# A written order of 431 steps for every engine, over units 0 to 8 of an attention and two-layer kernel

## The chip, the cores and the metric

One core of a Trainium2 chip runs the program. The metric is device time in microseconds, the median of repeated executions. The engines are TensorE (PE; its weight loads are PEld), VectorE (DVE), ScalarE (ACT), GpSimd (POOL) and SyncE (SP), which here only issues DMAs. Each engine works through its own instructions strictly in the order in which they stand in its list, and waits for the others by semaphores.

## What is computed

```python
q_pool = q.reshape(B, H, S // 2, 2, D).mean(axis=3)          # B 4, H 8, S 1152, D 64
scores = (1 / sqrt(D)) * q_pool @ k.transpose(0, 1, 3, 2)    # 576 x 1152 per head
attn = softmax(scores)                                       # maximum taken off first, sum + 1e-9
x = (attn @ v) as [2304 tokens, 512]
h = x @ w_in                                                 # 512 x 2048
g = where(h >= 1, h, where(h <= -1, 0, (h + 1) ** 2 / 4))
y = g @ w_out                                                # 2048 x 512
out = maximum(y @ w1, y @ w2, y @ w3) @ w_out2               # 512 x 768 (three), 768 x 512
```

Weights arrive as 64-bit floats; q, k and v as 32-bit floats.

## The kernel before

The attention is cut into 48 units (b, i, p): batch, third of the pooled queries (192 of them), pair of heads. A unit has three score groups, named by `who` 0, 1 and 2: 128 queries of one head, 128 of the other, and the last 64 of both. For each group PE makes 128 x 1152 scores `sc` (line 371), DVE takes the row maximum into `st` (385), ACT scales it (386) and takes the exponential into `pf` with the row sum in `sm` (387). PE turns `pf` in nine pieces into `tr` (423), ACT copies that to `pt` (434, 436), and PE multiplies `pt` with v (`av`, 454). Score and turned tiles share two places of three PSUM banks each (`place`, 148); all else that PE writes there shares two banks of the tag `g1`. `shares` (393) makes 1/sum: DVE inverts `sm`, POOL spreads it into `rb`, PE turns it (403, 404) into the tail of the place that holds `tr` of group 2, and ACT copies it to `R` (406, 407). Only then is that place free for a new `sc`. DVE multiplies `av` with `R` into `xf` (472); after four units the batch row block becomes `xh`, and the dense work begins: `ph` (523) with w_in and `py` (546) with w_out, eight `ph` and four `py` to a block of 192 tokens. `py` needs every half of w_out.

Beside the first units the weights are made. w_in comes in eight chunks of 1 MB (`raw_in`, 185), w_out in eight chunks of two loads of 512 KB each. ACT makes a chunk's absolute value (161), DVE turns it to 32 bits in four instructions (162, 163, 165, 167), ACT squares it for a norm (199, 252), and when the scale is known ACT and DVE make a high and a low half of 16 bits (153, 154). For w_out the scale needs the norms of all eight chunks and a turn on PE, `max_ou` (108). Five of the chunks of w_out, the third and the last four, are loaded into one tile `raw_ou` (238), so each of these loads waits until the second DVE instruction of line 167 of the one before has ended. k (and q) of a pair are squared on ACT (285), summed over partitions on PE (101), scaled and split on POOL and DVE (274, 275), and turned by a DMA into `kst` (and `qst`); v of batch 0 is used whole.

Before the change PE alone has a written order: the table `ORDER` gives the words of a unit, for the first 12 units

```python
"s0 w0 r d s1 d w1 t0 a1 q t1 w2 s2 d d w3 t2"
```

with `s` the scores and softmax of a group, `t` its turn, `r` 1/sum of the unit before, `a1` the `av` of the unit before, `d` one step of the dense work (from unit 5 on), `w` one step of the weights, which `W_AT` admits at some places only, and `q` the next q. `K0` and `V0` say at which group k and v of batch 0 take a step. PE's instructions stand as these words make them. The lists of the other engines are arranged by the framework's own scheduler, which goes by priorities; `shift(OW)` moves the weights' priority back.

Of the kernel before, what the change touches and what calls it, by code (L numbers as in the profile page):

```python
# [50 lines left out]
def body(ctx: ExitStack, tc: tile.TileContext, q, k, v, w_in, w_out, w1, w2, w3, w_o2, out):  # L51
# [28 lines left out]
    @contextmanager  # L80
    def shift(n):
        n = max(n, -tc.cur_priority)
        tc.cur_priority += n
        yield
        tc.cur_priority -= n

# [83 lines left out]
    def w_in_steps():  # L170
# [4 lines left out]
        HF = FF // 2  # L175

        f32 = wou.rearrange("p a b c d -> p (a b c d)").bitcast(F32)
        sqs = wou.rearrange("p a b c d -> p (a b c d)")[:, NF * DM:].rearrange("p (k f) -> p k f", k=KD).bitcast(BF16)
        raws = []

        def fetch(n):
            if n < 2 * KD:
                kt, h = divmod(n, 2)
                raw = gp.tile([P, HF, 2], U32, tag="g", name=f"raw_in{kt}_{h}")
                issued["w"] = load_q.dma_start(out=raw, in_=words(w_in[kt * P:(kt + 1) * P, h * HF:h * HF + HF])).ins
                raws.append(raw)

        fetch(0)
        yield
        fetch(1)  # L190
        yield
        for kt in range(KD):
            st = f32[:, kt % 2 * FF:(kt % 2 + 1) * FF]
            for h in range(2):
                c = slice(h * HF, h * HF + HF)
                raw = raws.pop(0)
                to_f32(st[:, c], raw)
                fetch(2 * kt + h + 2)
                nc.scalar.activation(out=sqs[:, kt, c], in_=st[:, c], func=AF.Square,
                                     accum_out=sq[:, 2 * kt + h:2 * kt + h + 1])  # L200
                if h == 0:
                    yield
            nc.vector.tensor_tensor(out=sr[:, kt:kt + 1], in0=sq[:, 2 * kt:2 * kt + 1], in1=sq[:, 2 * kt + 1:2 * kt + 2],
                                    op=ALU.add)
            root_scale(u_in[:, kt:kt + 1], s[:, kt:kt + 1], sr[:, kt:kt + 1], 1)
            for h in range(2):
                c = slice(h * HF, h * HF + HF)
                split_rows(win[:, 0, kt, c], win[:, 1, kt, c], st[:, c], s[:, kt:kt + 1])
            yield

        ps = psg.tile([P, 512], F32, tag="g1", name="sum_in")
        for kt in range(KD):
            for c in range(4):
                nc.tensor.matmul(ps[32 * c:32 * c + 32], ones16, sqs[:, kt, c * 512:(c + 1) * 512],
                                 start=(kt == 0), stop=(kt == KD - 1))
        nc.vector.tensor_reduce(out=um[:, 2:3], in_=ps, axis=AX.X, op=ALU.max)
# [3 lines left out]
        all_max(U_in, um, 2, "in")  # L220
        yield

    def w_ou_steps():
        NG = NF // 2
        mx = small.tile([P, NG], F32, tag="wsq", bufs=1, name="mx_ou")
        um = small.tile([P, 2], F32, tag="um", bufs=1, name="um_ou")
        s = small.tile([P, 1], F32, tag="wsc2", bufs=1, name="s_ou")
        f32 = wou.rearrange("p a b c d -> p a (b c d)").bitcast(F32)

        sts = [f32[:, h + 1] for h in range(NG - 1)]  # L230
        one = gp.tile([P, 6, DM], U32, tag="g", name="raw_ou")
        sts.append(one[:, 4:6].rearrange("p a b -> p (a b)").bitcast(F32))
        raws = {}

        def fetch(h):
            at_ = {0: 6, 1: 4, 3: 6}.get(h)
            if at_ is None:
                raw = one[:, 0:4].rearrange("p (a c) b -> p a (c b)", c=2).rearrange("p a (b c) -> p a b c", c=2)
            else:
                raw = wou[:, at_:at_ + 2].rearrange("p a b c d -> p a (b c d)").bitcast(U32).rearrange(  # L240
                    "p a (b c) -> p a b c", c=2)
            for f in range(2):
                ff = 2 * h + f
                load_q.dma_start(out=raw[:, f], in_=words(w_out[ff * P:(ff + 1) * P, :]))
            raws[h] = raw

        for h in range(3):
            fetch(h)
        yield
        for h in range(NG):  # L250
            to_f32(sts[h], raws.pop(h).rearrange("p a b c -> p (a b) c"))
            nc.scalar.activation(out=wou[:, 0, 0].bitcast(BF16), in_=sts[h].rearrange("p (a b) -> p a b", a=2),
                                 func=AF.Square, accum_out=mx[:, h:h + 1])
            for x in {0: (3,), 2: (4,), 4: (5,), 5: (6,), 6: (7,)}.get(h, ()):
                fetch(x)
            yield
        nc.vector.tensor_reduce(out=um[:, 0:1], in_=mx, axis=AX.X, op=ALU.max)
        root_scale(um[:, 1:2], s, um[:, 0:1], 1)
        all_max(U_ou, um[:, 1:2], 1, "ou")
        nc.vector.reciprocal(out=s, in_=U_ou)  # L260
        for h in range(NG):
            split_rows(wou[:, h, 0], wou[:, h, 1], sts[h].rearrange("p (a b) -> p a b", a=2), s)
            if h % 2:
                yield
# [7 lines left out]
    def split(hi, lo, x, s):  # L272

        nc.gpsimd.tensor_scalar(out=hi, in0=x, scalar1=s, scalar2=1.0, op0=ALU.mult, op1=ALU.mult)  # L274
        nc.vector.scalar_tensor_tensor(out=lo, in0=x, scalar=s, in1=hi, op0=ALU.mult, op1=ALU.subtract)

# [5 lines left out]
    def norm(n, junk, j, b, p, key):  # L282

        sq = small.tile([P, 1], F32, tag="sq", bufs=2, name=f"sq{key}{b}_{p}")
# [3 lines left out]
        root_scale(ub[b][:, p, j:j + 1], sb[b][:, p, j:j + 1], all_add(sq, 1, f"{key}{b}_{p}"), 1)  # L288

    def k_steps(b, p):  # L290

        if p == 0:
            ub[b] = small.tile([P, NPAIR, 2], F32, tag="ub", bufs=3, name=f"ub{b}")
            sb[b] = small.tile([P, NPAIR, 2], F32, tag="sb", name=f"sb{b}")
# [6 lines left out]
        split(kp[:, :, 0], kp[:, :, 1], kn.rearrange("p a b c -> p (a b) c"), sb[b][:, p, 0:1])  # L301
# [3 lines left out]
    def v_steps(b, p):  # L305

        if WHOLE(b, p):
# [6 lines left out]
            yield  # L314
# [6 lines left out]
        split(vv[:, 0], vv[:, 1], vn.rearrange("p a b c -> p (a b c)"), sb[b][:, p, 1:2])  # L321
        yield

    def q_prep(b, i, p):
# [543 lines left out]
```

## Time and profile before

| what | value |
|---|---|
| median of 3 runs | 1209.26 us (1209.18 to 1212.24) |
| the profiled execution | 1203.48 us |
| its span in the trace | 1201.7 us |
| mean granted clock of TensorE over the span | 0.956 |
| busy over the span: PE, DVE, ACT, POOL | 1074.7, 822.1, 739.6, 139.1 us |
| first `py` of the dense work | 229.65 us after the span's start |

Times in the trace count from the start of the span; the profiled execution is 1.8 us longer than its span, and 5.8 us shorter than the median of the runs. A window of the trace gives each engine's busy time and the granted clock of TensorE in it, where 1.00 is 2.4 GHz and a stretch in between mixes 2.4 and 1.2 GHz. The first maximum of a unit (line 385) marks where a unit begins below.

### The profile page before, as it was taken

The page shows a single profiled execution, that of the slowest core. Times are in us where ns is not written, and L with a number is a line of the kernel's source. Part 1 is how long each engine was busy: PE and PEld are TensorE (multiplying, and loading weights), DVE is VectorE, ACT ScalarE, POOL GpSimd, SP SyncE. Part 2 cuts the span into 40 slices and gives each one's busy share as a digit, 9 for nine tenths or more (in the row PEclk, how much of TensorE's full clock was granted, in tenths as well). Part 3 has the DMA queues.
Part 4 walks back from the last instruction along what each step waited for, and adds up shares of the span by engine and source line. Part 5 has one row for each costly group of instructions (what it writes and reads, how often), then busy time and mean ns, then how long its engine had stood idle before and what let it go on. Part 6 is the DMA issues. An engine that isn't in the chain of part 4 may idle for free.

```text
span 1201.7 us, 26667 instructions
## 1 busy us (share of the span) xinstructions
PE 1074.7 (89%) x11061; PEld 883.2 (73%) x11061; DVE 822.1 (68%) x1404; ACT 739.6 (62%) x1337; POOL 139.1 (12%) x160
## 2 busy tenths in 40 slices
PE   3557787899899988999999899998988999999998
PEld 2344566778788877788878788887986876777774
DVE  4976866668788888888889988786998551422220
ACT  4875777677777877777877888776474311112111
POOL 1110002112011121110112200000401020100000
PEclk9768889899999999999999999999988999999999
DMA  7854232247766689865589765556444120000001
GB/s 236 250 157 132 80 127 54 70 103 153 145 113 115 120 175 183 172 114 113 113 169 192 154 101 100 100 92 161 139 155 138 41 69 27 10 19 19 19 18 45
DMA packets 273754, 134.91 MB, mean 112 GB/s; under 512 B 229088, under 2 KB 256736, under 8 KB 272608
## 3 DMA queue, kind: packets, MB, share of 16 engines
q1 hardware_dynamic: 273632, 133.20, 48.8%
q8 instruction: 87, 1.43, 0.5%
q14 instruction: 35, 0.29, 0.1%
HBM read 62.39 MB, written 9.44 MB: 60 GB/s over the span
## 4 chain that ended last, share of the span: by engine, by line
PE 44%; DVE 4%; ACT 3%; issue 3%; DMA 3%; POOL 0%; ACTq 0%; SPq 0%; POOLq 0%; DVEq 0%
PE p L767 18%; PE py L546 7%; PE po L784 5%; PE ph L523 5%; PE sc L371 4%; PE av L459 3%; PE tr L423 1%; DMA pt<-hl 1%; DVE st L385 1%; ACT pf L387 1%; PE por L798 1%; ACT hl L440 1%; DVE st_m L167 1%; DVE hl L441 0%; DMA raw_m<-in_moe_w_dram 0%
## 5 line engine op out<-in xcount | busy, mean ns | idle before, releaser
L385 DVE TENSOR_REDUCE st<-sc 128x1 f32<-128x1152 f32 x144 | 194.6, 1351 | 45.5 <-PE sc L371 45.1
L767 PE MATMUL p<-yh,wm 128*128 128x288 f16 x1728 | 217.9, 288 | 5.7 <-ACT py L550 3.2
L371 PE MATMUL sc<-kst,qst 128*64 128x512 f16 (+3 forms) x1152 | 177.0, 341 | 39.3 <-ACT R L407 17.6
L546 PE MATMUL py<-g,wou 128*128 128x192 f16 x2304 | 204.3, 250 | 7.6 <-DVE xf L472 4.2
L767 PEld LDWEIGHTS <-wm 128*128 128x128 f16 x1728 | 170.2, 99 | 53.1 <-issue 7.0
L546 PEld LDWEIGHTS <-wou 128*128 128x128 f16 x2304 | 195.2, 100 | 15.9 <-issue 15.0
L523 PE MATMUL ph<-xh,win 128*128 128x192 f16 x2304 | 203.9, 249 | 3.2 <-POOL xh L274 2.1
L523 PEld LDWEIGHTS <-win 128*128 128x128 f16 x2304 | 195.2, 99 | 5.9 <-issue 3.5
L387 ACT ACTIVATE pf<-sc,st,esc 128x1152 f32<-128x1152 f32 x144 | 188.8, 1311 | 5.8
L371 PEld LDWEIGHTS <-qst 128*64 128x64 f16 (+1 forms) x1152 | 84.6, 108 | 99.7 <-issue 42.5
L423 PE MATMUL tr<-ident,pf 128*128 128x128 f32 x648 | 97.9, 304 | 50.4 <-ACT pf L387 50.4
L423 PEld LDWEIGHTS tr<-ident,pf 128*128 128x128 f32 x648 | 82.0, 158 | 61.7 <-ACT pf L387 55.4
L441 DVE TENSOR_TENSOR hl<-pf,hl 128x1152 f16<-128x1152 f32 x72 | 100.2, 1391 | 13.4 <-ACT hl L440 10.7
L775 ACT ACTIVATE h<-mx 128x288 f16<-128x288 f32 x48 | 21.2, 443 | 133.5 <-DVE mx L773 133.5
L772 DVE TENSOR_TENSOR mx<-p,mx 128x288 f32<-128x288 f32 x48 | 21.9, 456 | 106.2 <-PE p L767 105.7
L459 PE MATMUL av<-pt,vhl 128*64 128x192 f16 x1944 | 87.1, 247 | 3.7 <-DMA pt<-hl 3.7
L459 PEld LDWEIGHTS <-vhl 128*64 128x64 f16 x1944 | 79.3, 110 | 13.4 <-issue 8.3
L386 ACT ACTIVATE st<-st,esc 128x1 f32<-128x1 f32 x144 | 41.6, 289 | 71.2 <-DVE st L385 70.7
L440 ACT ACTIVATE hl<-pf 128x1152 f16<-128x1152 f32 x72 | 83.1, 1154 | 0.0
L531 DVE SCALAR_TENSOR_TENSOR g<-t,dgs,g 128x384 f16<-128x384 f32 x96 | 62.3, 653 | 5.0 <-ACT g L530 4.9
L784 PE MATMUL po<-wo,h 128*128 128x512 f16 x288 | 64.3, 379 | 0.0
L430 DVE TENSOR_TENSOR pt<-tr,pt 128x1152 f16<-128x1152 f32 x36 | 48.8, 1356 | 18.8 <-ACT pt L429 18.8
(171 smaller groups left out, 1267.3 us busy)
## 6 DMA issues: line engine op xcount, KB each, us to landing
kn<-in_k_dram SPq DMA_DIRECT2D x16, 576.0 KB, 4.4
vn<-in_v_dram SPq DMA_DIRECT2D x16, 576.0 KB, 4.3
raw_m<-in_moe_w_dram SPq DMA_DIRECT2D x12, 768.0 KB, 4.5
raw_in<-in_moe_w_in_dram SPq DMA_DIRECT2D x8, 1024.0 KB, 5.9
qn<-in_q_dram SPq DMA_DIRECT2D x24, 256.0 KB, 3.4
raw_ou<-in_moe_w_out_dram SPq DMA_DIRECT2D x10, 512.0 KB, 4.4
qst<-qst SPq DMA_DIRECT2D x48, 96.0 KB, 2.2
y_d<-ys SPq DMA_DIRECT2D x48, 96.0 KB, 2.0
```

The costliest lines, as they stand in the source:

```text
L371: nc.tensor.matmul(sc[m0:m1, n0:n1], qst[b, i, p][who][:, var, m0:m1], ks[:, h, n0:n1], start=(var == 0), stop=(var == 1))
L385: nc.vector.tensor_reduce(out=m, in_=sc, axis=AX.X, op=ALU.max, negate=True)
L387: nc.scalar.activation(out=pf, in_=sc, func=AF.Exp, bias=nb, scale=e, accum_out=sums[b, i, p][:, who:who + 1])
L423: nc.tensor.transpose(tr[:, c * P:(c + 1) * P], pf[:, c * P:(c + 1) * P], ident)
L440: nc.scalar.activation(out=hl[:, 0], in_=pf, func=AF.Copy)
L441: nc.vector.tensor_tensor(out=hl[:, 1], in0=pf, in1=hl[:, 0], op=ALU.subtract)
L459: nc.tensor.matmul(acc[64 * h:64 * h + 64], vhl[b, p][:, vi, h, c, :], pt[:, h, pi * KT + c, :], start=(c == 0 and e == 0), stop=(c == KT ...
L523: nc.tensor.matmul(ph[:, a], win[:, wi, kt, ff * P:(ff + 1) * P], x[:, xi, kt], start=(kt == 0 and e == 0), stop=(kt == KD - 1 and e == 2))
L531: nc.vector.scalar_tensor_tensor(out=g[:, 1, fs, :], in0=t2, scalar=gs, in1=g[:, 0, fs, :], op0=ALU.mult, op1=ALU.subtract)
L546: nc.tensor.matmul(py, wou[:, ff // 2, wi, ff % 2, m * P:(m + 1) * P], g[:, gi, ff, :], start=(ff == 0 and e == 0), stop=(ff == NF - 1 and ...
L767: nc.tensor.matmul(ph[:, :NB2], wm[:, wi, i, kt, ff * P:(ff + 1) * P], yh[:, yi, kt, n0:n0 + NB2], start=(kt == 0 and e == 0), stop=(kt == ...
L784: nc.tensor.matmul(po, h2t[b][:, hi, ff, t * P:(t + 1) * P], wo[:, wi, ff, :], start=(ff == 0 and e == 0), stop=(ff == NF2 - 1 and e == 2))
```

## The change

Units 0 to 8 are no longer made by `ORDER`. A string `OPENING` of 431 steps names pieces of work, and each mention of a piece runs it to its next `yield`: `v0` to `v3` and `k0` to `k3` (v and k of batch 0), `q0` to `q8`, `w0` to `w7` and `wi` (chunks of w_in, and its scale), `o0` to `o7` and `oo` (chunks of w_out, and its scale), `sNW` (group W of unit N, from the scores to the copy into `pt`), `rN` (1/sum), `aN` (`av`), `x0`, `x1` (`xh` of a block) and `u00` to `u06` (the first seven `ph` of the dense work). While this runs, PE, ACT, DVE, POOL and SP all take their instructions in the order in which the steps make them; the scheduler may still put instructions of later units between them, and does on ACT, DVE, POOL and SP. 1/sum of these units is turned into a bank of the tag `g1` (`rs`), no longer into the tail of `tr`. The scaled maximum of these units is made on DVE. From unit 9 on the table `ORDER` goes on without the words for the weights; seven `ph` are done by then, before it was eight.

```diff
+OTHERS = {mybir.EngineType.Activation, mybir.EngineType.DVE, mybir.EngineType.Pool, mybir.EngineType.SP}
+FROM = 9
+FIRST = lambda b, i, p: b == 0 and 4 * i + p < FROM
+NB_DVE = (0, 1, 2)
+OPENING = """
+v0 v1 q0 v2 v3 v0 k0 q2 v0 v1 v0 q0 v1 w0 v1 w1 q0 k1 v2 q0 q0 v2 v3 q0 v2 q0 v3 k0 v3 q4 q2 k0 k0 q2 k0 q2 w0
...
+r7 s72 o4 s80 r7 s81 s80 o4 o5 a7 s81 s80 s80 s81 a7 x1 x1 u05 s80 o5 x1 s81 u05 o5 s82 s81 u05 u06 s82 u05 u05
+s82 o5 u06 o5 o6 s82 u06 s82 u06 u06 o6 o6 o6 o7 o6 o7 o7 o7 o7 oo oo oo o0 o0 o1 o1 o2 o2 o3 o3 o4 o4 o5 o5 o6
+o6 o7 o7
+"""
...
     def soft(b, i, p, who):
...
+        sc = qk(b, i, p, who)
+        yield
...
+        nc.vector.tensor_reduce(out=m, in_=sc, axis=AX.X, op=ALU.max, negate=True)
+        if FIRST(b, i, p) and who in NB_DVE:
+            nc.vector.tensor_scalar(out=nb, in0=m, scalar1=e, scalar2=PS, op0=ALU.mult, op1=ALU.add)
+        yield
+        if not (FIRST(b, i, p) and who in NB_DVE):
+            nc.scalar.activation(out=nb, in_=m, func=AF.Copy, scale=e, bias=PS)
         pf = pfp.tile([P, KT * P], F32, tag="pf", name=f"pf{key}")
...
+        yield from turned(b, i, p, who, pf)
...
     def shares(b, i, p):
...
+        rs = R[b, i, p] if not FIRST(b, i, p) else psg.tile([P, 512], F32, tag="g1", name=f"rs{b}_{i}_{p}")
         nc.tensor.transpose(rs[:, 0:P], rb.rearrange("p a o -> p (a o)"), ident)
...
+    def opening():
+
+        gens = {}
+        for name in OPENING.split():
+            if name not in gens:
+                gens[name] = piece(name)
+            run(gens[name], 1)
+        for name in gens:
+            run(gens[name])
...
     order = tc.manual_schedule(engines=ORDERED)
     order.__enter__()
...
+    with tc.manual_schedule(engines=OTHERS):
+        opening()
+    for t in range(3 * FROM):
+        now(t)
...
+    for n, (b, i, p) in list(enumerate(units))[FROM:]:
```

Where the change moves instructions, three places, as the built programs list them. Names carry unit and group: `sc0_0_1_0` is group 0 of unit (0, 0, 1).

PE at the end of unit 0, before:

```order
L371 MATMUL sc0_0_0_2_237<-kst0_0_125,qst0_0_0_149 64x128
L423 MATMUL tr0_0_0_2_278<-ident_80,pf0_0_0_2_251 128x128 x9
L371 LDWEIGHTS qst0_0_0_149
L371 MATMUL sc0_0_1_0_291<-kst0_1_181,qst0_0_0_149 128x512
L371 LDWEIGHTS qst0_0_0_149
```

and in the change:

```order
L394 MATMUL sc0_0_1_0_353<-kst0_1_229,qst0_0_0_188 128x128
L106 MATMUL sum_k0_3_377<-sqk0_3_367,ones_78 128x1
L458 MATMUL tr0_0_0_2_384<-ident_80,pf0_0_0_2_375 128x128 x9
L458 MATMUL tr0_0_1_0_402<-ident_80,pf0_0_1_0_382 128x128 x9
L433 MATMUL rs0_0_0_416<-ident_80,rb0_0_0_400 128x128
L434 MATMUL rs0_0_0_416<-ident_80,sm0_0_0_281 128x128
```

The turn of group 2 stood right behind its scores; now the scores of the next unit's group 0 stand between, two turns follow each other, and 1/sum goes to a tile of its own.

DVE from the first chunk of w_in to the first two maxima, before:

```order
L162 TENSOR_SCALAR wou_74<-wou_74 128x1024
L163 TENSOR_SCALAR wou_74<-wou_74 128x1024
L165 SCALAR_TENSOR_TENSOR wou_74<-raw_in0_0_157,wou_74 128x1024
L167 SCALAR_TENSOR_TENSOR wou_74<-raw_in0_0_157,wou_74 128x1024
L385 TENSOR_REDUCE st0_0_0_0_172<-sc0_0_0_0_165 128x1
L385 TENSOR_REDUCE st0_0_0_1_193<-sc0_0_0_1_186 128x1
```

and in the change, behind the whole first chunk and the first half of the second:

```order
L173 SCALAR_TENSOR_TENSOR wou_74<-raw_in0_1_165,wou_74 128x1024
L175 SCALAR_TENSOR_TENSOR wou_74<-raw_in0_1_165,wou_74 128x1024
L282 SCALAR_TENSOR_TENSOR kpre0_1_228<-kn0_1_170,sb0_123,kpre0_1_228 128x18x64
L207 TENSOR_TENSOR sr_in_157<-sq_in_156 128x1
L98 TENSOR_SCALAR u_in_77<-sr_in_157 128x1
L100 TENSOR_SCALAR u_in_77<-u_in_77 128x1
L101 RECIPROCAL s_in_158<-u_in_77 128x1
L379 SCALAR_TENSOR_TENSOR esc0_0_0_279<-ub0_122,sqq0_0_0_168 128x1
L409 TENSOR_REDUCE st0_0_0_0_282<-sc0_0_0_0_258 128x1
L411 TENSOR_SCALAR st0_0_0_0_282<-st0_0_0_0_282,esc0_0_0_279 128x1
L409 TENSOR_REDUCE st0_0_0_1_287<-sc0_0_0_1_272 128x1
```

Two chunks and the second k stand ahead of the first maximum, where one chunk stood, and the scaled maximum follows each maximum.

PE around the turn of w_out's scale, before (in unit 7):

```order
L454 MATMUL av0_1_2_1462<-pt_0_1_2_1258,vn0_2_434 64x192 x18
L423 MATMUL tr0_1_3_1_1499<-ident_80,pf0_1_3_1_1409 128x128 x9
L108 MATMUL max_ou_1514<-ident_80,um_ou_890 128x128
L371 LDWEIGHTS qst0_1_2_1094
L371 MATMUL sc0_1_3_2_1522<-kst0_3_437,qst0_1_2_1094 64x512
```

and in the change (behind unit 8):

```order
L567 MATMUL ph0_0_6_1621<-xh0_0_996,win_73 128x192
L458 MATMUL tr0_2_0_2_1660<-ident_80,pf0_2_0_2_1651 128x128 x9
L113 MATMUL max_ou_1695<-ident_80,um_ou_1689 128x128
L394 LDWEIGHTS qst0_2_0_1095
L394 MATMUL sc0_2_1_0_1720<-kst0_1_229,qst0_2_0_1095 128x512
```

The turn now stands behind the last group of unit 8, right ahead of the first scores of unit 9. The eight low halves of w_out (line 154, now 258) had all stood ahead of unit 9's first maximum in DVE's list; in the change one stands ahead of it and seven behind.

## Rows read from the trace of the kernel before

**Rows 1.** Stretches: span, length, busy PE, PEld, DVE, ACT, POOL, PEclk, DMA share, GB/s.

```profile
20.10:40.00 19.90, 13.36 (x57) 9.18 (x55) 16.49 (x27) 17.13 (x26) 1.52 (x2) 0.84 1.02 345
40.00:131.50 91.50, 55.19 (x382) 38.69 (x382) 69.74 (x137) 64.13 (x100) 12.35 (x15) 0.76 0.50 143
131.50:217.90 86.40, 65.20 (x551) 52.28 (x552) 59.57 (x98) 65.87 (x107) 10.48 (x13) 0.86 0.30 90
217.90:229.65 11.75, 11.75 (x124) 9.74 (x123) 6.57 (x11) 9.19 (x16) 1.00 (x1) 0.99 0.12 36
229.65:800.00 570.35, 543.74 (x6723) 478.15 (x6723) 475.97 (x775) 443.30 (x834) 78.32 (x99) 0.99 0.70 135
```

**Rows 2.** Waits of PE up to 215.7 us: total us, times, longest.

```profile
PE tr L423 <- ACT pf L387: 43.8, 14, 8.9
...
PE sc L371 <- ACT R L407: 8.0, 3, 4.0
```

**Rows 3.** Timeline of PE in 185:206: start, us, instructions, idle time before.

```profile
185.50 1.20 PE L423 MATMUL tr<-ident,pf 128*128 128x128 f32 x9
...
191.13 2.18 PE L423 MATMUL tr<-ident,pf 128*128 128x128 f32 x9 [3.22 <-ACT pf L387]
193.10 1.69 PE L371 MATMUL sc<-kst,qst 128*128 128x512 f16 x6
...
199.18 1.14 PE L371 MATMUL sc<-kst,qst 128*128 128x512 f16 x6 [2.17 <-ACT R L407]
```

**Rows 4.** Timeline of DVE at the start.

```profile
6.88 0.15 DVE L95 TENSOR_SCALAR ub<-ub 128x1 f32<-128x1 f32 x1
7.07 0.16 DVE L96 RECIPROCAL sb<-ub 128x1 f32<-128x1 f32 x1
...
9.02 1.42 DVE L275 SCALAR_TENSOR_TENSOR kpre<-kn,sb,kpre 128x1152 f16<-128x1152 f32 x1
10.93 0.62 DVE L275 SCALAR_TENSOR_TENSOR qpre<-qn,sqq,qpre 128x384 f16<-128x384 f32 x1 [0.49 <-POOL qpre L274]
11.46 0.69 DVE L162 TENSOR_SCALAR wou<-wou 128x1024 f32<-128x1024 f32 x1
...
14.17 1.22 DVE L167 SCALAR_TENSOR_TENSOR wou<-raw_in,wou 128x1024 uint32<-128x1024 uint32 x1
20.10 1.36 DVE L385 TENSOR_REDUCE st<-sc 128x1 f32<-128x1152 f32 x1 [4.71 <-PE sc L371]
```

**Rows 5.** Timeline of DVE in 50:60.

```profile
51.46 1.27 DVE L154 SCALAR_TENSOR_TENSOR win<-wou,s_in,win 128x1024 f16<-128x1024 f32 x1
52.65 0.68 DVE L163 TENSOR_SCALAR wou<-wou 128x1024 uint32<-128x1024 uint32 x1
...
58.25 1.34 DVE L385 TENSOR_REDUCE st<-sc 128x1 f32<-128x1152 f32 x1
59.52 1.20 DVE L165 SCALAR_TENSOR_TENSOR wou<-raw_in,wou 128x1024 uint32<-128x1024 uint32 x1
```

**Rows 6.** Timeline of DVE in 164:175.

```profile
165.76 1.22 DVE L167 SCALAR_TENSOR_TENSOR wou<-raw_ou,wou 128x1024 uint32<-128x1024 uint32 x1
166.90 0.61 DVE L531 SCALAR_TENSOR_TENSOR g<-t,dgs,g 128x384 f16<-128x384 f32 x1
167.43 0.55 DVE L529 SCALAR_TENSOR_TENSOR t<-t 128x384 f32<-128x384 f32 x1
167.90 0.41 DVE L472 SCALAR_TENSOR_TENSOR xf<-av,Uv,R 128x192 f32<-128x192 f32 x1
...
173.07 0.69 DVE L162 TENSOR_SCALAR raw_ou<-raw_ou 128x1024 f32<-128x1024 f32 x1 [1.32 <-ACT raw_ou L161]
```

**Rows 7.** Timeline of ACT in 164:175.

```profile
171.90 1.14 ACT L161 ACTIVATE raw_ou<-raw_ou 128x1024 f32<-128x1024 f32 x1 [0.56 <-DMA raw_ou<-in_moe_w_out_dram]
```

**Rows 8.** Page, costliest groups: the scaled maximum on ACT.

```profile
L386 ACT ACTIVATE st<-st,esc 128x1 f32<-128x1 f32 x144 | 41.6, 289 | 71.2 <-DVE st L385 70.7
```

**Rows 9.** Timeline of ACT at the start.

```profile
4.75 1.16 ACT L285 ACTIVATE kpre<-kn 128x1152 bf16<-128x1152 f32 x1 [2.74 <-DMA kn<-in_k_dram]
```

More of the change, by code (lines that the diff above doesn't have):

```diff
@@ L219, in w_in_steps @@
         yield
-        all_max(U_in, um, 2, "in")
+        yield from all_max(U_in, um, 2, "in")
         yield
-    def w_ou_steps():
-        NG = NF // 2
-        mx = small.tile([P, NG], F32, tag="wsq", bufs=1, name="mx_ou")
-        um = small.tile([P, 2], F32, tag="um", bufs=1, name="um_ou")
[L227 to L248, printed above, removed]
-        yield
[L250 to L259, printed above, removed]
@@ L260, in w_ou_steps, with w_ou_last @@
+    def w_ou_last():
+        um = small.tile([P, 2], F32, tag="um", bufs=1, name="um_ou")
+        s = w_s["ou"] = small.tile([P, 1], F32, tag="wsc2", bufs=1, name="s_ou")
+        nc.vector.tensor_reduce(out=um[:, 0:1], in_=w_s["mx"], axis=AX.X, op=ALU.max)
+        root_scale(um[:, 1:2], s, um[:, 0:1], 1)
+        yield
+        yield from all_max(U_ou, um[:, 1:2], 1, "ou")
         nc.vector.reciprocal(out=s, in_=U_ou)
[L261 to L264, printed above, removed]
+        yield
@@ new lines, in down_step @@
+        for ff in range(NF):
+            for e, (wi, gi) in enumerate(((0, 0), (0, 1), (1, 0))):
+                nc.tensor.matmul(py, wou[:, ff // 2, wi, ff % 2, m * P:(m + 1) * P], g[:, gi, ff, :],
+                                 start=(ff == 0 and e == 0), stop=(ff == NF - 1 and e == 2))
+        yield
+        ys = tp.tile([P, NB], F32, tag="ys", bufs=1, name=f"ys{b}_{i}_{m}")
+        nc.scalar.activation(out=ys, in_=py, func=AF.Copy, scale=gd)
+        nc.scalar.activation(out=py, in_=py, func=AF.Square, scale=gd, accum_out=y2[:, b, i, m:m + 1])
@@ L554, in dense_steps @@
+        copy_q.dma_start(out=y_d[b][:, m, i * NB:(i + 1) * NB], in_=ys)
+        yield
+    begun = set()
     def dense_steps(units):
-        down = iter(())
+        down = []
         for b, i in units:
-            for k, _ in enumerate(up_steps(b, i)):
-                yield
-                if k % 2 == 1:
-                    next(down, None)
+            for k in range(NF // 2):
+                if ("u", b, i, k) not in begun:
+                    run(up_step(b, i, k))
                     yield
-                    yield
-            down = down_steps(b, i)
@@ L565, in dense_steps @@
-        for _ in down:
+                if k % 2 == 1 and down:
+                    job = down.pop(0)
+                    if ("y", *job) not in begun:
+                        run(down_step(*job))
+                        yield
+                        yield
+            down = [(b, i, m) for m in range(NM)]
+        for job in down:
+            run(down_step(*job))
             yield
             yield
-    def run(gen):
-        for _ in gen:
-            pass
     dense = dense_steps([(b, i) for b in range(B) for i in range(NBL)])
-    def w_steps():
-        yield from w_in_steps()
-        yield from w_ou_steps()
```

368 lines of the change are left out of this document (213 added, 155 removed).

## The prediction

> **What bounds the kernel now.** I read first the busy time by stretches. Behind the first `py`, at 229.65 us, PE is busy for 543.74 of 570.35 us, 95%; before it, in units 1 to 8, for 55.19 of 91.50 and 65.20 of 86.40 us, 60% and 75% [rows 1]. From the first `py` on PE's list is the same in both kernels but for the `ph` done ahead, so what the change is worth is by how much the first `py` moves. Next come the waits of PE ahead of it: the largest by far is that for the exponential, `tr` on `pf`, 43.8 us in 14 waits; `sc` on `R` has 8.0 in 3 [rows 2]. The timeline of PE shows the pattern: scores of one group, a turn that must wait 3.22 us for that group's maximum and exponential, the next scores, a wait of 2.17 us for `R` [rows 3]. Last, DVE: it is busy 69.74 of 91.50 and 59.57 of 86.40 us [rows 1], the busiest engine in the first and, behind PE and ACT, not far off in the second. So a unit lasts as long as DVE's instructions in it, plus what a serial round leaves open.
>
> I sum DVE's list with prices taken from start to start, since neighbours overlap a little: a small instruction 0.19 us (6.88 to 7.07); a chunk of weights 3.93 (11.46 to the end of its fourth instruction, 14.17 + 1.22), the low half of a k 1.42, of a q 0.53 [rows 4]; a 16-bit half of a chunk 1.19 (51.46 to 52.65), a maximum 1.27 (58.25 to 59.52) [rows 5]; one `g` 0.53, one second step of `t` 0.47, one `xf` 0.33 of its 0.41 as an estimate [rows 6]. Units 1 to 4 of before hold 12 maxima (15.2), 72 small (13.7), 16 half chunks of two instructions (31.4), 8 halves (9.5) and 6.8 of the rest: 76.6 of 91.5 us. Units 5 to 8 hold 61.2 of 86.4. What is left is 14.9 and 25.2 us: **the overhead of a unit is 3.7, then 6.3 us**, 5.0 on average. These are the two numbers that the change can alter.
>
> **The change part by part.**
>
> *The written order.* In units 1 to 7 DVE's new list holds 21 maxima (26.7), 21 scaled maxima and 69 other small ones (17.1), ten chunks (38.8), seven halves (8.3) and 13.7 of the rest (a k, four q, seven `xf`, an `xh`, five steps of the dense work): **104.6 us**. Scores now go in pairs: two in flight, then two turns, so that one group's maximum and exponential lie beside the other's turn and copy. Three rounds of a unit become one and a half, even units with one pair and odd ones with two. I take the overhead as halved with them: 1.85 a unit for units 1 to 4, 3.15 for 5, 6, 7 and 9, in all 7.4 + 12.6 = **20.0 us**. Bounds: nothing at all below, and 6.3 a unit above, as in units 5 to 8 now; I take the half because the count of rounds is what changes.
>
> *1/sum in its own bank.* The 8.0 us of `sc` on `R` [rows 2] lie in the overhead that was halved; nothing more is counted. Covering it is the next wait, that for `pf`. The bank is one of the two of `g1`, which the sums of k and v, `av` and `ph` share; each of those is held for one copy, so a delay is bounded by a unit's overhead, above.
>
> *Scaled maximum on DVE.* 27 instructions at 0.19 are 5.1 us more on DVE, in the sums above. ACT loses 27 at 0.289 [rows 8], 7.8 us, hidden: in units 1 to 8 it has 130.0 us of busy time [rows 1], and loses 7.0 of them, against DVE's 104.6 + 25.3 in the new list. If ACT has no slack left, these 7 us are a gain, inside the lower bound.
>
> *The start.* On SP four loads of v and q of units 0 and 1 now stand ahead of k. A v is 1152 x 128 x 4 bytes, 0.59 MB; with q some 2.6 MB go first, at the 345 GB/s of the stretch 20.1 to 40 [rows 1] 7.5 us. The square of k started at 4.75 [rows 9] and the first maximum at 20.10 [rows 4], 15.35 later, so it now comes near 27.6. On DVE two chunks and the second k's half stand ahead of it, 9.3 us, of which one chunk was there before and fitted. Unit 0 then holds only 11.6 us on DVE (three maxima, one chunk, one k, one half and seven small), so unit 1 begins at 27.6 + 11.6 + 0.8, **40.0**, as before [rows 1]. Bounds 38 and 46 (two overheads of 3.7 less the 0.8 and the second chunk not hidden).
>
> *The tail of w_out.* Here the written order costs something. The last four chunks use one tile, `raw_ou`. A reload is seen: DVE's last reader ends at 165.76 + 1.22 = 166.98, its next instruction on the tile starts at 173.07 [rows 6], **6.1 us** later, of which ACT's absolute value, 1.14 from 171.90 [rows 7], is the end. Now DVE had dense steps and a maximum in that gap; in the new list unit 8's work ends and chunks 5, 6 and 7 follow each other with `max_ou` behind, and on PE `max_ou` stands ahead of unit 9's scores, so nothing passes. From the end of chunk 4, just ahead of unit 8's first maximum, DVE has 13.0 us up to the end of chunk 5 (unit 8's three maxima among it); chunk 6 costs 6.1 + 3.9 and chunk 7 the same; the norm's small instructions, the turn of 0.27 and the hops between I put at 3.2, and the first scores and half of unit 9 at 2.3, both estimates. With 1.1 of overhead unit 8 lasts 13.0 + 20.0 + 3.2 + 2.3 + 1.1 - 0.5 = **39.1 us**, where it lasted 23. A reload that lands at once cannot be less than ACT's 1.14, which makes the lower bound 29; two loads of 0.5 MB behind a k and a v of the next batch, 1.2 MB at 345 GB/s, would wait 3.4 more each, the upper one 49.
>
> *Unit 9.* Up to the last half of w_out, which the first `py` needs, DVE holds 16.8 us: seven halves, three maxima, dense steps. The one more `ph` on PE lies in waits there.
>
> **Sum.** 40.0 + 104.6 + 20.0 + 39.1 + 16.8 = 220.5: the first `py` 9.1 us earlier. The profiled execution took 1203.48 us, 5.8 less than the median 1209.26 of the runs; on the median the forecast is **1200.2 us**. Its own bounds, with the terms a few us to either side, are 1193 to 1208.
>
> **TensorE's clock.** A turn of nine took 1.20 us at 185.50 and 2.18 behind the wait of 3.22; the granted clock is 0.76 and 0.86 in units 1 to 8 and 0.99 behind [rows 1, 3], so it mixes 1.2 and 2.4 GHz there. Each wait that makes the following turn and scores slow costs up to 0.98 + 0.55 (1.69 against 1.14) [rows 3]. The Trainium skill ("TensorE: Matmul & The Clock Gate", section "Part 1: The HAM clock gate") says that throttled is the default and that activity releases it; the rows agree. By that rule pairs without waits would gain these 1.5 us in each of some twelve rounds, 18 us, and the time would be near 1182, as in the first rival below. The sum above leaves it out, since the overhead that it would come from is already halved there.
>
> **The rivals.**
> *Much faster, chance 0.20.* The pairs overlap fully: overhead zero, so the first `py` at 200.5 and the time near 1180. For it: PE's waits for `pf` are 43.8 us [rows 2], more than all overhead, and the clock rises with them gone. Against it: DVE's own order is now fixed, with each instruction in line behind the next late one.
> *No change, 0.20.* The mechanism is the reloads with other loads ahead, 3.4 us more on three: the first `py` at 230.7, 1.1 late, time 1208 to 1211. For it: the DMA engines are shared by one queue, and at the start it is full (share 1.02 [rows 1]). Against: in 131.5 to 217.9 the share is 0.30.
> *Slower, 0.24.* The overhead is not halved but stays: DVE works its list strictly in order, a late maximum holds the ready weights behind it as before, and with the scaled maximum there is one more instruction that can be late in each group. 40.1 us instead of 20.0 puts the first `py` at 240.6, 10.9 late: 1220. Its place is `tr` on `pf` in units 1 to 7. It decides at 29.1 us of overhead for the eight units, 3.6 each, 73% of today's: above that the tail's 16 us outweigh all that the pairs give. At 6.3 a unit it would be 1230.
> *The change does not do what it says, 0.04, in the slower and equal cases.* Instructions of later units still stand between the written ones on ACT and DVE (a q of batch 1 in unit 8); each is one of the prices above and moves the time by 1 to 2 us only.
>
> **How the numbers follow.** The forecast has 0.36, the faster rival 0.20, no change 0.20, slower 0.24. A measurement of this kernel can tell about 0.3%, 3.6 us, from no change: faster is below 1205.6, slower above 1212.9. Faster: all of the fast rival and the forecast, 0.56; same 0.20; slower 0.24. Signs are mixed, so the range reaches from the fast rival to the slow one, **1179 to 1220**, with a tenth left out on each side.
>
> **What would show it.** Right: the first maxima near 27.6 (unit 0) and 40 (unit 1); unit 8's first maximum near 40 + 104.6 + 17 = 161 and unit 9's near 201; three idle times of DVE on `raw_ou` of about 5 us each at the end of unit 8 and a long wait of PE at `max_ou`; the first `py` near 220; `tr` on `pf` down to some 20 us; no `sc` on `R` before unit 9. Wrong: unit 8's first maximum past 170 (overhead not halved), `max_ou` not waiting (tail hidden), a first maximum past 32, or a stretch behind the first `py` that is not 1201.7 - 229.65 = 972 us long, which would mean that the 972 depend on more than PE's list.

## The result and the profile after

The changed kernel took 1222.81 us (median of 4 runs, 1221.76 to 1225.68) against 1209.22 us before (1202.89 to 1212.24): the ratio is 1.0123, with a 95% interval of 1.0079 to 1.0167. It is slower, 13.6 us by the medians, where 9 us faster were forecast. The profiled execution took 1221.76 us; its span is 1220.0 us, 18.3 longer than before, and the mean granted clock of TensorE is 0.964.

The stretches of the changed kernel come first (span, length, busy PE, PEld, DVE, ACT, POOL with counts, granted clock, DMA share, GB/s). They are cut at the first maxima of units 1, 8, 9, 10, 20 and 47, so the rows answer to those of [rows 1]:

```profile
0.00:43.93 43.93, 15.41 (x64) 9.96 (x64) 29.12 (x59) 26.91 (x39) 13.09 (x15) 0.92 1.02 307
43.93:148.87 104.94, 87.52 (x782) 66.76 (x783) 101.35 (x188) 91.47 (x136) 13.96 (x16) 0.95 0.46 129
148.87:190.26 41.39, 15.40 (x138) 12.13 (x139) 25.68 (x48) 20.06 (x31) 6.30 (x8) 0.68 0.33 107
190.26:215.75 25.49, 21.45 (x207) 17.99 (x205) 20.16 (x28) 21.28 (x32) 1.51 (x2) 0.92 0.29 66
215.75:381.10 165.35, 154.53 (x1839) 133.81 (x1839) 127.52 (x215) 124.56 (x230) 23.00 (x29) 1.00 0.61 120
381.10:833.45 452.35, 410.95 (x5029) 356.39 (x5028) 365.75 (x569) 337.54 (x621) 56.61 (x70) 0.98 0.65 126
833.45:1220.00 386.55, 362.53 (x3014) 276.76 (x3012) 174.80 (x330) 121.56 (x223) 28.54 (x20) 0.98 0.20 64
```

And the kernel before, cut at the first maxima of units 1, 8, 10, 20 and 47:

```profile
39.97:194.83 154.86, 104.65 (x796) 78.56 (x797) 111.81 (x205) 112.16 (x179) 15.03 (x20) 0.80 0.44 129
...
235.77:396.70 160.93, 153.56 (x1839) 133.87 (x1839) 125.21 (x215) 122.54 (x232) 21.94 (x29) 1.00 0.66 130
396.70:816.99 420.29, 401.05 (x5029) 353.49 (x5028) 360.14 (x569) 330.57 (x621) 55.45 (x70) 0.99 0.71 135
816.99:1201.70 384.71, 365.52 (x3014) 279.04 (x3012) 174.25 (x330) 121.25 (x223) 30.21 (x20) 0.97 0.21 66
```

The reader should compare pairs. Units 1 to 7 take 104.94 us, where they took 154.86, with the clock at 0.95 where it was 0.80. Unit 8 alone then takes 41.39 us with PE busy for 15.40 of them. Unit 10 begins at 215.75 us; it began at 235.77, so at this point the change is **20.0 us ahead**. Then look at units 20 to 46: the same 5029 matmuls take 452.35 us where they took 420.29, **32.1 us more**; units 10 to 19 take 4.4 more, and what follows unit 47's first maximum 1.8 more. 32.1 + 4.4 + 1.8 = 38.3, less the 20.0, is the 18.3 us by which the span grew. Nearly all of the loss lies in units that the written order does not contain.

The waits of PE in the first 300 us of the changed kernel (total, times, longest) answer to [rows 2]:

```profile
PE max_ou L113 <- DVE um_ou L100: 22.6, 1, 22.6
PE tr L458 <- ACT pf L416: 18.3, 11, 4.3
...
PE sc L394 <- ACT R L439: 2.6, 2, 1.9
...
PE py L592 <- DVE wou L258: 2.9, 2, 1.9
```

`tr` on `pf` is down from 43.8 to 18.3 us. Of the 2.6 us of `sc` on `R` none lies before unit 10; [rows 2] has 8.0. In their place stands one wait of 22.6 us for `max_ou`, the turn behind which the scale of w_out is known.

What grew is seen in the timeline of PE in a late unit (start, us, instructions, idle time before it and what ended it). Before, in unit 40:

```profile
715.24 1.15 PE L423 MATMUL tr<-ident,pf 128*128 128x128 f32 x9
716.23 4.12 PE L523 MATMUL ph<-xh,win 128*128 128x192 f16 x48
720.19 0.27 PE L403 MATMUL tr<-ident,rb 128*128 128x128 f32 x1
720.30 0.27 PE L404 MATMUL tr<-ident,sm 128*128 128x128 f32 x1
720.41 1.14 PE L371 MATMUL sc<-kst,qst 128*128 128x512 f16 x6
```

In the changed kernel, the same place of its own unit 40:

```profile
725.31 1.15 PE L458 MATMUL tr<-ident,pf 128*128 128x128 f32 x9
726.30 2.14 PE L567 MATMUL ph<-xh,win 128*128 128x192 f16 x24
729.16 0.30 PE L433 MATMUL tr<-ident,rb 128*128 128x128 f32 x1 [0.72 <-DVE pt L467]
729.30 0.27 PE L434 MATMUL tr<-ident,sm 128*128 128x128 f32 x1
729.41 1.14 PE L394 MATMUL sc<-kst,qst 128*128 128x512 f16 x6
730.48 2.42 PE L500 MATMUL av<-pt,vhl 128*64 128x192 f16 x54
732.73 1.14 PE L394 MATMUL sc<-kst,qst 128*64 128x512 f16 x12
733.80 2.15 PE L567 MATMUL ph<-xh,win 128*128 128x192 f16 x24
735.79 3.38 PE L592 MATMUL py<-g,wou 128*128 128x192 f16 x39
```

The window ends inside the last `py`, at 39 of its 48 matmuls.

Between the turn of group 2 and 1/sum (the two small `tr` of `rb` and `sm`) there were 48 matmuls of `ph`, two steps of the dense work, 4.12 us long. Now there are 24, 2.14 us, and PE waits 0.72 us; the other `ph` stands further down, ahead of `py`. In these batches PE turns group 2 alone; ACT takes the high half of the turned tile out of PSUM, and DVE behind it the low half. What PE waits for is that second reading, first before and then in the change:

```profile
717.60 1.36 DVE L430 TENSOR_TENSOR pt<-tr,pt 128x1152 f16<-128x1152 f32 x1 [0.79 <-ACT pt L429]
```

```profile
727.66 1.36 DVE L467 TENSOR_TENSOR pt<-tr,pt 128x1152 f16<-128x1152 f32 x1 [0.79 <-ACT pt L466]
```

It starts 2.35 us after the turn has begun on PE (727.66 against 725.31) and ends at 729.02; before it was 2.36 us (717.60 against 715.24). With two `ph` in between PE comes to 1/sum after its end; with one it comes before. Over units 20 to 46 this wait, absent from the list of waits before, is in total the largest of PE in the changed kernel (total, times, longest):

```profile
PE tr L433 <- DVE pt L467: 24.2, 24, 4.3
```

Why one `ph` is missing there was in the text of the change. Each unit from 9 on takes four dense steps by its words, and a `py` takes two of them, the second empty. From unit 12 on, `d d` stand ahead of `r` and `d d` at the end. With eight `ph` done ahead, unit 9 began a new block, and in the later batches the words fell as "`ph` `ph` r ... `py` -". With seven done, all later steps are one word late: "- `ph` r ... `ph` `py`". The phase never comes right again.

### The profile page after: what moved, and what is told of

Its sections match the earlier page's. It is cut to its first block, busy times and chain, and to the rows that moved or that the text cites. A ratio compares the mean times of both kernels' runs of the same rounds, so it can differ in the third digit from the quotient of the medians.

```text
span 1220.0 us, 26675 instructions
## 1 busy us (share of the span) xinstructions
PE 1067.8 (88%) x11061; PEld 873.8 (72%) x11061; DVE 844.4 (69%) x1431; ACT 743.4 (61%) x1310; POOL 143.0 (12%) x160
## 5 line engine op out<-in xcount | busy, mean ns | idle before, releaser
L592 PE MATMUL py<-g,wou 128*128 128x192 f16 x2304 | 200.8, 248 | 13.2 <-ACT g L576 6.3
L592 PEld LDWEIGHTS <-wou 128*128 128x128 f16 x2304 | 192.3, 98 | 15.4 <-issue 10.0
L567 PEld LDWEIGHTS <-win 128*128 128x128 f16 x2304 | 191.2, 98 | 12.1 <-issue 10.4
L394 PE MATMUL sc<-kst,qst 128*64 128x512 f16 (+3 forms) x1152 | 171.3, 335 | 21.2 <-ACT pf L416 8.8
L458 PE MATMUL tr<-ident,pf 128*128 128x128 f32 x648 | 90.2, 290 | 18.6 <-ACT pf L416 18.3
L500 PE MATMUL av<-pt,vhl 128*64 128x192 f16 x1944 | 94.3, 259 | 2.9 <-DMA pt<-hl 2.9
L458 PEld LDWEIGHTS tr<-ident,pf 128*128 128x128 f32 x648 | 76.4, 150 | 28.0 <-ACT pf L416 18.5
L500 PEld LDWEIGHTS <-vhl 128*64 128x64 f16 x1944 | 86.4, 117 | 13.6 <-issue 10.5
L576 ACT ACTIVATE g<-t,dgs 128x384 f16<-128x384 f32 x96 | 58.6, 613 | 39.3 <-DVE t L574 39.0
L578 DVE SCALAR_TENSOR_TENSOR g<-t,dgs,g 128x384 f16<-128x384 f32 x96 | 66.4, 694 | 19.2 <-ACT g L576 18.8
L573 DVE TENSOR_SCALAR t<-t 128x384 f32<-128x384 f32 x96 | 42.6, 444 | 32.5 <-ACT t L571 30.7
```

The source lines that it names most:

```text
L394: nc.tensor.matmul(sc[m0:m1, n0:n1], qst[b, i, p][who][:, var, m0:m1], ks[:, h, n0:n1], start=(var == 0), stop=(var == 1))
L458: nc.tensor.transpose(tr[:, c * P:(c + 1) * P], pf[:, c * P:(c + 1) * P], ident)
L500: nc.tensor.matmul(acc[64 * h:64 * h + 64], vhl[b, p][:, vi, h, c, :], pt[:, h, pi * KT + c, :], start=(c == 0 and e == 0), stop=(c == KT ...
L567: nc.tensor.matmul(ph[:, a], win[:, wi, kt, ff * P:(ff + 1) * P], x[:, xi, kt], start=(kt == 0 and e == 0), stop=(kt == KD - 1 and e == 2))
L578: nc.vector.scalar_tensor_tensor(out=g[:, 1, fs, :], in0=t2, scalar=gs, in1=g[:, 0, fs, :], op0=ALU.mult, op1=ALU.subtract)
L592: nc.tensor.matmul(py, wou[:, ff // 2, wi, ff % 2, m * P:(m + 1) * P], g[:, gi, ff, :], start=(ff == 0 and e == 0), stop=(ff == NF - 1 and ...
```

## The experiments

Eleven kernels. The columns are the first maximum of unit 10, the length of units 20 to 46 (first maximum of 20 to that of 47, us, in the profile), and the median with its ratio to the kernel before and 95% interval. Each ratio is to the runs of the kernel before on the same chip; their medians lie between 1207.51 and 1209.29 us.

| kernel | unit 10 at | units 20 to 46 | median us | ratio |
|---|---|---|---|---|
| before | 235.77 | 420.3 | 1209.22 | 1 |
| the change | 215.75 | 452.4 | 1222.81 | 1.0123 (1.0079 to 1.0167) |
| e1 eighth ph | 220.00 | 426.2 | 1185.44 | 0.9819 (0.9788 to 0.9849) |
| e2 words | 217.76 | 426.2 | 1190.07 | 0.9866 (0.9822 to 0.9909) |
| e3 before, a step late | 240.71 | 458.4 | 1254.01 | 1.0376 (1.0339 to 1.0412) |
| e4 eighth ph, ACT | 220.41 | 424.6 | 1187.23 | 0.9840 (0.9802 to 0.9878) |
| e5 bank all | 218.51 | 437.2 | 1204.98 | 0.9973 (0.9954 to 0.9992) |
| e6 no reload | 212.39 | 425.3 | 1180.99 | 0.9786 (0.9750 to 0.9822) |
| e7 PE order only | 236.67 | 421.6 | 1210.06 | 1.0020 (0.9997 to 1.0042) |
| e8 unit 9 in tail | 212.27 | 426.9 | 1196.74 | 0.9906 (0.9869 to 0.9942) |
| e9 q early | 197.35 | 425.3 | 1187.57 | 0.9824 (0.9795 to 0.9852) |
| e10 eighth ph early | 217.90 | 423.4 | 1186.78 | 0.9807 (0.9778 to 0.9835) |
| e11 eighth ph, bank all | 219.24 | 428.1 | 1197.65 | 0.9902 (0.9876 to 0.9928) |

**Phase or lists: e1, e2, e3.** The rival to the phase was that the scheduler leaves other lists on ACT, DVE and POOL behind a written opening. e1 does the eighth `ph` in the opening:

```diff
-s82 o5 u06 o5 o6 s82 u06 s82 u06 u06 o6 o6 o6 o7 o6 o7 o7 o7 o7 oo oo oo ...
+s82 o5 u06 o5 o6 s82 u06 s82 u06 u06 u07 o6 u07 o6 u07 o6 o7 u07 o6 u07 o7 o7 o7 o7 oo oo oo ...
```

> The change with the eighth ph of the first block done in the opening (in the wait for max_ou), so that unit 9 starts as in the kernel before. Theory A (phase): from unit 9 on the seven instead of eight ph shift the dense work by one step against the words of a unit; one ph instead of two stands between the turn of group 2 and 1/sum, PE waits there, and a unit of the later batches takes 15.42 us instead of 14.51. Then units 36 to 47 are 14.5 us apart again and the time is 1185 to 1193 us. Theory B (lists): the later units are slower because of how the scheduler left the lists of ACT, DVE and POOL behind a written opening; then units stay 15.4 us apart and the time is 1220 to 1226 us.

e2 keeps seven, and moves the words of the later batches by one step:

```diff
-         False: "s0 t- d d r s1 t0 a1 s2 t1 q d d"}
+         False: "s0 t- d d d r s1 t0 a1 s2 t1 q d"}
```

> The change with seven ph in the opening as it is, but the words of a unit of batches 1 to 3 moved by one dense step, so that two ph stand ahead of 1/sum again. Theory A: units 36 to 47 are 14.5 us apart, the time is 1185 to 1195 us. Theory B: 15.4 us apart, 1220 to 1226 us.

e3 takes the kernel before and leaves one dense step of unit 5 out, so that it is one step late for good:

```diff
-            if n >= DENSE:
+            if n >= DENSE and (n, late) != (DENSE, []):
                 next(dense, None)
+            elif n == DENSE:
+                late.append(n)
```

> The kernel before with one dense step left out in unit 5, so that only seven ph are done ahead and all later dense work is one step late; nothing else changes. Theory A: its later units become 15.4 us apart, and the time is 1240 to 1250 us. Theory B: its units stay 14.5 us apart, and the time is 1207 to 1213 us.

The expectation of e3 speaks of seven `ph`. In its trace eight are done ahead of unit 9, as in the kernel before; the step that is short is an empty one, and the order alone is shifted.

e1 and e2 fell into the range of the phase, 1185.44 and 1190.07 us; e3 came out at 1254.01, 4 us past its range and far from the other. Their rows for units 20 to 46, e1 and then e3:

```profile
379.46:805.66 426.20, 404.40 (x5029) 356.08 (x5028) 360.25 (x570) 330.36 (x621) 54.91 (x70) 0.98 0.71 133
```

```profile
409.10:867.52 458.42, 413.11 (x5029) 357.69 (x5028) 367.27 (x569) 338.38 (x621) 56.27 (x70) 0.97 0.64 124
```

One step of the order is worth 38 us in the kernel before (420.3 against 458.4 us in these units alone) and 26 us in the changed one. The spacing of maxima was expected at 14.5 against 15.4 us; within units 40 to 47 it is 14.59 in e1 and 15.42 in the change (102.16 and 107.94 us for seven). Times 27 units that is 22 of the 26 us; the units at the turn from one batch to the next add the rest. PE in e1's unit 40 has the two `ph` together again, and no wait; below it a late unit of e3, in which PE waits the same 0.72 us:

```profile
703.29 1.15 PE L458 MATMUL tr<-ident,pf 128*128 128x128 f32 x9
704.28 4.12 PE L567 MATMUL ph<-xh,win 128*128 128x192 f16 x48
708.24 0.27 PE L433 MATMUL tr<-ident,rb 128*128 128x128 f32 x1
```

```profile
728.52 1.15 PE L423 MATMUL tr<-ident,pf 128*128 128x128 f32 x9
729.51 2.14 PE L523 MATMUL ph<-xh,win 128*128 128x192 f16 x24
732.38 0.30 PE L403 MATMUL tr<-ident,rb 128*128 128x128 f32 x1 [0.72 <-DVE pt L430]
```

**The wait itself: e5, e11.** 1/sum goes into the same place as the turn. e5 is the change with 1/sum of all units in a bank of its own:

```diff
-        rs = R[b, i, p] if not FIRST(b, i, p) else psg.tile([P, 512], F32, tag="g1", name=f"rs{b}_{i}_{p}")
+        rs = psg.tile([P, 512], F32, tag="g1", name=f"rs{b}_{i}_{p}")
...
-            if who == 2 and not FIRST(b, i, p):
-                R[b, i, p] = rs
```

> The change (seven ph ahead) with 1/sum of all 48 units in a bank of its own, not of the first nine alone. It asks which wait makes a unit 15.4 us long. Theory 1/sum: PE waits only because the turn of 1/sum goes into the place whose copy to pt is not done; in its own bank the wait (0.72 us a unit) is gone, units 36 to 47 are 14.5 to 14.8 us apart and the time is 1190 to 1200 us. Theory place: the next scores, right behind it on PE, need that same place, so they wait instead; units stay 15.3 to 15.5 us apart and the time is 1218 to 1226 us.

1204.98 us, between the two ranges. The wait has moved to the next scores, which need the place itself:

```profile
PE sc L394 <- DVE pt L465: 15.5, 25, 2.8
```

15.5 us instead of 24.2, and units 20 to 46 take 437.2 us, half of the way back. So both hold: the place keeps PE, and 1/sum in it keeps PE longer. e11 makes the same edit to e1, where nothing waits for the place:

> e1 with 1/sum of all 48 units in its own bank, as in e5. With two ph ahead of 1/sum nothing waits for the place any more, so the bank has no wait to take away: 1183 to 1188 us. If 1/sum in the bank in itself is quicker (or the bank it takes delays ph and av), the time is below 1181 or above 1190 us.

A miss: 1197.65 us, 12.2 more than e1. The first list below is of units 20 to 46, the second from 800 us on:

```profile
PE av L498 <- ACT t L569: 17.3, 6, 4.7
```

```profile
PE sum_y L106 <- DVE ezs L801: 8.7, 1, 8.7
```

In units 20 to 46 `av` now waits for ACT to read a `ph`, which shares the banks of `g1`; the wait of `sc` for `R`, 9.9 us in e1, is gone, and these units take 1.9 us more. Of the 9.4 us by which the span is longer (1196.1 against 1186.7) 7.5 lie behind unit 47's first maximum, where PE waits once for 8.7 us at the last stage's `sum_y`. e1 does not show that wait, and e5, with the same bank, has 0.9 us of it, so its cause stays open.

The four kernels also price the phase with and without the place. In units 20 to 46 the step that is late costs 26.2 us with 1/sum in the place (452.4 against 426.2) and 9.1 with the bank (437.2 against 428.1); by the medians it is 37.4 and 7.3 us. Most of what the phase costs hangs on where 1/sum goes.

**The tail of w_out: e6, e8, e9, e10.** e6 is e1 without the loads of the last three chunks; the fourth last is used in their place, so this part of w_out is other data.

```diff
-        for f in range(2):
+        for f in range(2 if h < 5 else 0):
```

> e1 without the loads of the last three chunks of w_out (the fourth last is used four times, so y is another): all instructions stay, only the wait for the reload of the one tile goes. If the reloads hold DVE as the prediction has it, the 10.8 us that DVE idles for them in e1 (2.09, 2.90 and 5.78) go, and the time is 1173 to 1177 us. If other work fills the place at once, 1183 to 1187 us.

1180.99 us, between the two. Unit 9 began at 186.73 instead of 194.43 us, and PE's wait for `max_ou` fell from 22.1 (e1, whose waits stand first) to 15.5:

```profile
PE max_ou L113 <- DVE um_ou L100: 22.1, 1, 22.1
PE tr L458 <- ACT pf L416: 19.5, 12, 4.3
```

```profile
PE max_ou L113 <- DVE um_ou L100: 15.5, 1, 15.5
```

Two thirds of this wait stay without any reload; what is left on DVE and ACT there is mostly the chunks' own work. e8 and e9 fill the tail with unit 9, e8 like this (its last lines are left out):

```diff
-FROM = 9
+FROM = 10
...
+s82 o5 u06 o5 o6 s82 s90 u06 r8 s82 u06 u06 r8 s90 s91 r8 s90 s82
+r8 o6 s91 o6 s91 a8 s90 o6 o7 o6 s91 s92 u07 s90 s92 s91 a8 s92 u07 q10 o7 u07 o7 s92 u07 o7 u07 o7 s92 oo oo oo
...
```

> e1 with unit 9 written into the opening too, its scores, turns and av between the reloads of w_out, ahead of max_ou. If PE's 22.1 us of waiting for max_ou is room for it, unit 10 begins 8 to 15 us earlier than at 220.0, of which 8.2 us of dense work that unit 9 no longer does come back later: 1176 to 1184 us. If the instructions of unit 9 hold up the chunks on DVE and ACT, 1188 us or more.

A miss: 1196.74 us, in the range given for chunks that are held up, but from another cause. `max_ou` was not later (at 189.53 us, in e1 at 190.98); the q of the next units came too late:

```profile
PE sc L395 <- DMA qst<-qpre: 18.0, 1, 18.0
PE max_ou L114 <- DVE um_ou L101: 6.5, 1, 6.5
```

e9 puts the steps of `q10` beside unit 7.

> e8 with the q of units 10 and 11 prepared beside unit 7 instead of at the end. In e8 PE waited 18.0 us for that q behind max_ou. If that alone undid e8, unit 10 begins at 194 to 203 us instead of 212.3 and the time is 1174 to 1184 us. If the chunks themselves come later because unit 9 stands between them, unit 10 begins past 208 us and the time is 1188 us or more.

Unit 10 then began at 197.35 us, 22.7 earlier than in e1, inside the range given; the time did not follow, a miss: 1187.57 us, the same as e1 within the intervals. Units 10 to 19 take 173.7 us instead of 159.5, so 14.2 of the 22.7 are lost there at once, with a granted clock of 0.96 instead of 1.00. `max_ou` stands at 193.66 us and the last half of w_out at 221.0, in e1 at 190.98 and 214.2, so here the weights do come later; whether this costs the 14.2 us was not tried. At unit 47 9.3 us are left (796.32 against 805.66), and of these 8.2 us are dense work that unit 9 no longer does and that is still to come: what follows takes 6.4 us more (387.4 against 381.0). e10 puts the eighth `ph` and its steps ahead of chunk 6:

```diff
-s82 o5 u06 o5 o6 s82 u06 s82 u06 u06 u07 o6 u07 o6 u07 o6 o7 u07 o6 u07 o7 o7 o7 o7 oo ...
+s82 o5 u06 o5 o6 s82 u06 u07 s82 u06 u07 u06 u07 u07 u07 o6 o6 o6 o7 o6 o7 o7 o7 o7 oo ...
```

> e1 with the eighth ph and its four steps on ACT and DVE all ahead of chunk 6 of w_out, in the first wait for a reload, instead of spread over chunks 6 and 7. In e1 unit 9 began at 194.43, in the change at 190.26. If the spread steps held the chunks up, unit 9 begins 2 to 4 us earlier than in e1, and the time is 1181 to 1184 us. If not, 1184 to 1188 us.

Unit 9 began at 192.08 us, 2.4 earlier, as for spread steps that hold the chunks up; the time, 1186.78 us, fell into the other range and can't be told from e1's.

**What makes the opening short: e4, e7.** e4 sets `NB_DVE = ()` in e1, e7 drops the written order of ACT, DVE, POOL and SP.

> e1 with the scaled maximum of units 0 to 8 back on ACT. By the sums of DVE's list, which lasts as long as the units of the opening, 27 small instructions less make the first py up to 5 us earlier than in e1. If instead the hop from DVE to ACT and ACT's own list count, it is 2 to 8 us later. The later units are as in e1.

Neither came: the first `py` is at 206.68 us instead of 206.16, the time is 1187.23 us. The place of the scaled maximum makes no difference that is seen.

```diff
-    with tc.manual_schedule(engines=OTHERS):
-        opening()
+    opening()
```

> e1 with the written order of the opening for PE alone; ACT, DVE, POOL and SP are arranged by the scheduler again. If PE's pairs are what shortens the units of the opening, the time is within 3 us of e1 (1182 to 1189 us). If the other engines' written lists are what does it, the units of the opening get their overhead of some 5 us each back, in part or in whole: 1195 to 1220 us.

1210.06 us, 25 us slower than e1, with the first `py` at 218.19. PE has the same pairs, but waits again for the exponential (up to 218 us):

```profile
PE tr L458 <- ACT pf L416: 38.3, 12, 7.3
```

38.3 us against e1's 19.5 above, and against 43.8 in the kernel before. Units 1 to 7 take 136.5 us, where they take 105.0 in e1 and took 154.9 before, and unit 1 begins at 49.37 us, 9.4 later than before; unit 10 comes at 236.67 us, as late as before. So PE's pairs alone keep a third of what units 1 to 7 won, and the later start and tail use it up: it takes the lists of the other engines, written to fit PE's pairs, to shorten the opening. Which of the four lists does it was not taken apart.

## Why the prediction was wrong

**The step that failed** is the first: "From the first `py` on PE's list is the same in both kernels but for the `ph` done ahead, so what the change is worth is by how much the first `py` moves." The exception in that sentence was the result. By it the stretch behind the first `py` was to stay at 972 us; it took 1016.4 (1220.0 - 203.60), one of the signs named for being wrong. How many dense steps are done ahead sets where every later one stands, and PE, busy for 95% of the time there, had little to spare: before, it came to 1/sum 4.95 us after the start of the turn (715.24 to 720.19), and DVE had read the turn 3.72 us after it (717.60 + 1.36). e1 to e3 show from both kernels that the phase is the cause; e5 shows that about half of its price goes when 1/sum leaves the place, and that the next scores then wait for the place (15.5 us). The forecast priced the missing `ph` as work ("lies in waits there") and never as a place in the order; the listing of PE's order for one late unit would have shown a single `ph` ahead of 1/sum, and the trace of before had the rest: one `ph` less, some 2 us, takes PE to 1/sum 3 us after the turn's start, too early by 0.7, and 0.72 us was the wait.

The rival that ended on the right side, 1220 us, was right in its number by chance: its mechanism, an overhead that stays in units 1 to 7, did not occur. None of the rivals held the phase.

**Start.** Unit 1 was to begin at 40.0 us and began at 43.93, inside the bound of 46; the first maximum of unit 0 came at 30.61, not 27.6.

**Units 1 to 7.** With DVE's 104.6 us and an overhead of 16.9 unit 8 would have begun at 161; it began at 148.87, 104.94 us behind unit 1. DVE is busy for 101.35 of these, where it was for 111.81 of 154.86: what it leaves open went from 43.1 to 3.6 us, not to a half. Here the fast rival was right. The prices of the prediction's list come out above the busy time, by 3 us here and by 7 in units 1 to 4 of before, where they make 76.6 us against 69.74 [rows 1]; by the busy time 21.8 us were open there, not 14.9, so more could be won than the sum allowed. (Ten chunks at 3.93 are 39.3 us, not 38.8.) The granted clock, a mix of 1.2 and 2.4 GHz, went along: 0.95 in units 1 to 7 with PE busy for 87.52 of 104.94 us, 0.80 before with 104.65 of 154.86, and 0.68 in unit 8 with 15.40 of 41.39. That agrees with the rule of the Trainium skill ("TensorE: Matmul & The Clock Gate", section "Part 1: The HAM clock gate") that the throttled state is the default and activity releases it.

**The tail** was right in size: unit 8 was to last 39.1 us and lasted 41.39, and PE waited 22.6 us at `max_ou`. From DVE's last instruction on chunk 5 to its first on chunk 6, and again to chunk 7, 6.15 and 6.06 us passed, 6.1 as forecast:

```profile
162.86 1.22 DVE L175 SCALAR_TENSOR_TENSOR wou<-raw_ou,wou 128x1024 uint32<-128x1024 uint32 x1
...
170.23 0.69 DVE L169 TENSOR_SCALAR wou<-wou 128x1024 f32<-128x1024 f32 x1 [2.79 <-ACT wou L167]
...
173.69 1.22 DVE L175 SCALAR_TENSOR_TENSOR wou<-raw_ou,wou 128x1024 uint32<-128x1024 uint32 x1
180.97 0.69 DVE L169 TENSOR_SCALAR raw_ou<-raw_ou 128x1024 f32<-128x1024 f32 x1 [6.05 <-ACT raw_ou L167]
```

But of three idle times of about 5 us there are 0.22 (ahead of chunk 5), 2.79 and 6.05, and e6 shows in e1 that without the reloads PE's wait shrinks by a third only: the rest of the tail is not the reloads. The chain of w_out hardly moved as a whole: `max_ou` is on PE at 186.77 us, where it was at 186.54. The written order took units from behind it to ahead of it, and 46.0 us gained at unit 8 (148.87 against 194.83) became 20.0 at unit 10.

**Unit 9** was to hold 16.8 + 3.2 us up to the first `py`; it came 13.3 after unit 9's first maximum, at 203.60 us, with the last half of w_out, up to which the forecast counted, ending at 211.89. Unit 10 began 12.2 us behind the first `py`, where it was 6.1 before. Of the 26.1 us by which the first `py` came earlier, 20.0 were left at unit 10, and from there the forecast's method would give 1189 us. e1, in which the phase is mended, tests that method: unit 10 begins 15.8 us earlier than before (220.00 against 235.77) and the span is 15.0 us shorter (1186.7 against 1201.7). By the medians it is 22.1 us, 1185.44 against 1207.51 on its chip.

**Scaled maximum and bank.** Both were forecast to change little by themselves, and e4 agrees for the first. For units 0 to 8 the bank was not taken out alone.

## What to carry to other kernels

A stretch that is bound by one engine and "has the same list" is only the same if every position in it is the same: when a change moves the number of steps done ahead of a repeating pattern, compare one late period instruction by instruction, and ask which short wait the moved piece was covering. A loss of about 1 us a unit over 38 units outweighed a gain of 20 us that was real and where it was sought. To test such a suspicion, shift the phase alone, in both kernels, and to keep the gain, fix the count of steps: with one more `ph` in the opening the written order is 1.8% faster than the kernel before.

## What was not expected of the hardware

No engine did anything new; a size surprised. PE at 95% busy looked saturated, yet moving one `ph` by a few places lengthened units 20 to 46 by 26 to 38 us with the same 5029 matmuls. From before to the change PE's idle time in them grew from 19.2 us (420.29 - 401.05) to 41.4 us (452.35 - 410.95), and its busy time by 9.9 us, with a granted clock of 0.98 instead of 0.99: the waits came with more than their own length. By these rounded clocks some 5 us of the 9.9 are slower clock, an estimate (0.02 of 452.35 us less 0.01 of 420.29); the rest stays open.
